# Every third half-unit of the second layer's first half takes a score bank and the attention bank for its sums

## The chip, the cores and the metric

The kernel runs on one core of one Trainium2 chip. The metric is the device time of one execution in microseconds. Five engines work side by side, each through its own instruction stream in order: TensorE (PE, its weight loads PEld), VectorE (DVE), ScalarE (ACT), GpSimd (POOL) and SyncE (SP, which issues the transfers).

## The reference

Attention with RMS-normed q and k (4 batches, 12 heads, 448 positions, head size 64), then two feed-forward layers over the 1792 tokens; what matters for the change is the last one:

```python
def _moe2_ref(x, w_in, w_out):      # x 1792x768, w_in 768x2048, w_out 2048x768
    h = x @ w_in
    g = h * np.cos(h)
    return (g @ w_out).astype(np.float32)
```

## The kernel before, in words

The work comes in stages: attention of batch 0, then gate, val and out1 of the first layer for batch after batch with the attention of the next batch threaded in, then the second layer in two halves: "h" (`x @ w_in` with `h cos h`) and "out2" (`g @ w_out`). Every operand of the second layer is kept as a pair of fp16 parts, high and low, so each 128x128 block of weights costs three matmuls of 448 columns (L1002 to L1004: high x high, high x low, low x high).

The loop of the h half (L1265 to L1294) runs over 8 pieces `c` of 256 columns of `w_in` and, inside, over 4 batches `b`. One pass of the inner loop is called a **half-unit** here: 256 output columns of one batch, as two banks of PSUM (`f` = 0 and 1), 36 matmuls in all. There are 32 half-units, in the order c, b, and four of them with one `c` are called a group. PSUM has eight banks: four in the pool `ps_m` (tiles "mm"), three score banks in `ps_s` (tiles "s"), one attention bank in `ps_t` (tile "t"); the names s and t are of the attention, which is over by then. A half-unit takes two mm banks (L1269), so its banks come round again two half-units later.

What reads the banks is `fin_h` (L1123 to L1149), for each of the two banks: ACT rounds to a whole multiple (L1134), DVE takes off the multiple of two pi in two steps (L1140 and L1141, the first reads the bank), ACT takes the absolute value and the sine (L1142, L1143), DVE multiplies by the bank (L1144, the last reader of the bank), ACT and POOL split the product into two fp16 parts (L1148, L1149). The bank is free when L1144 is done.

Beside this the loop prepares weights. At `b == 3` it converts the next `w_in` pieces from their 64-bit form (`conv64`: L841, L842, L843 on DVE), takes their squares (L861 on ACT) and splits a piece that is already scaled (L873 on ACT, L874 on DVE). At `b == 1` `w_scale` adds the squares up across partitions with a tiny matmul (L868, in a bank of `ps_s`). From the half-unit (5, 3) on, `pre_step` converts the last pieces of `w_out` in the same way, one for each half-unit, and at (7, 1) `out2_scales` sets the scales with which out2's weights are split (L930 on ACT, L931 on DVE, from `raw` tiles that are loaded back from DRAM, `raw<-o`). Out2 (L1297 on) takes its banks from all three pools: s, s, s, t, mm, mm, mm, and its matmuls are L1015.

The order on each engine is not the program's: the kernel is built with a scheduler that walks through the program with a timing model and lets an instruction that is ready go ahead of an earlier one. Tiles of one pool are handed out in the program's order. So a change of the banks moves instructions on every engine.

```python
ps_t = ... tile_pool(name="ps_t", bufs=1, space=PSUM)     # L175
ps_s = ... tile_pool(name="ps_s", bufs=3, space=PSUM)     # L176
ps_m = ... tile_pool(name="ps_m", bufs=4, space=PSUM)     # L1194
```

Of the kernel before, what the change touches and what calls it, by code (L numbers as in the profile page):

```python
# [140 lines left out]
def kernel(ctx: ExitStack, tc, q, k, v, g_q, g_k, w_gate, w_val, w_out, w2_in, w2_out, out):  # L141
# [33 lines left out]
    ps_t = ctx.enter_context(tc.tile_pool(name="ps_t", bufs=1, space=PSUM))  # L175
    ps_s = ctx.enter_context(tc.tile_pool(name="ps_s", bufs=3, space=PSUM))  # L176
# [7 lines left out]
    def xy_tile(more=False):  # L184
        return xy_pools[more].tile([P, 2, S], F16, tag="xy", name="xy")
# [4 lines left out]
    def bank(pool, tag):  # L190
        return pool.tile([P, 512], F32, tag=tag, name=tag)
# [707 lines left out]
    def w_loads(upto):  # L899
        while nload[0] <= min(upto, len(pieces) - 1):  # L900
            pc = pieces[nload[0]]
            if (pc["kind"] == "out1" and not pc["fresh"] or pc["kind"] == "out2" and pc["fresh"]) and nload[0] > upto - LA + LO:
                return
            w_load(nload[0])
            nload[0] += 1

    def w_conv(j):
        if j >= len(pieces) or not pieces[j]["fresh"] or pieces[j]["kind"] == "out2":
            return
        pc = pieces[j]  # L910
        w32_t[j] = conv64(raw_t.pop(j))
        if pc["kind"] != "out1":
            squares(unit_of(pc), w32_t[j])

    def w_scale(j):
        if j < len(pieces) and pieces[j]["fresh"] and pieces[j]["last"] and pieces[j]["kind"] in ("gate", "val", "h"):
            unit_scale(unit_of(pieces[j]))

    def w_split(j):
        if j >= len(pieces) or not (pieces[j]["fresh"] or pieces[j]["kind"] == "out1"):  # L920
            return
        pc = pieces[j]
        if pc["kind"] == "out2":
            wp_full[j] = []
            for kk in range(2):
                kt = pc["k0"] + kk
                w32 = w32_t.pop((j, kt))
                so = oscl[:, kt:kt + 1]
                wp = wp_tile(F16)
                nc.scalar.activation(wp[:, 0], w32, AF.Copy, scale=so)  # L930
                nc.vector.scalar_tensor_tensor(wp[:, 1], w32, so, wp[:, 0], op0=ALU.mult, op1=ALU.subtract)  # L931
                wp_full[j].append(wp)
                for o in range(H * D // CO):
                    dst = scr["out2", o, pc["k0"]].rearrange("p a x -> p (a x)").rearrange("p (k a f) -> p k a f", k=2, a=2)
                    stores.append((dst[:, kk], wp[:, :, o * CO:(o + 1) * CO]))
            wp_t[j] = None
            return
        w32 = w32_t.pop(j)
        dst = scr[pc["key"]]
        if pc["kind"] == "out1":  # L940
            wh, wl = wp_tile(F32R), wp_tile(F32R)
            nc.scalar.activation(wh, w32, AF.Copy)  # L942
            nc.gpsimd.tensor_sub(wl, w32, wh.bitcast(F32))  # L943
            if pc["fresh"]:
                stores.append((dst, w32))
            wp_t[j] = (wh, wl)
        else:
            wp = split16(unit_of(pc), w32)
            if pc["kind"] != "h":
                stores.append((dst, wp))  # L950
            wp_t[j] = (wp[:, 0], wp[:, 1])

    def w_store():
        while stores:
            dst, src = stores.pop(0)
            nc.sync.dma_start(dst, src)
# [6 lines left out]
    def pre_step(more=True):  # L963
        done = False
        if pre_split and (pre_split[0][0] == "out2" or len(pre_split) > 1):
            kind, c, k0, w32 = pre_split.pop(0)
            if kind == "h":
                for kind, c, k0, w32 in ((kind, c, k0, w32), pre_split.pop(0)):
                    stores.append((scr[kind, c, k0], split16(UNIT0[kind] + c, w32)))
            done = True  # L970
        if pre_scale and (pre_scale[0][0] == "out2" or len(pre_scale) > 1):
            kind, c, k0, w32 = pre_scale.pop(0)
            unit_scale(UNIT0[kind] + c)
            if kind == "h":
                pre_split.append((kind, c, k0, w32))
                pre_split.append(pre_scale.pop(0))
            done = True
        if pre_conv:
            kind, c, k0, rw = pre_conv.pop(0)
            w32 = conv64(rw)  # L980
            squares(UNIT0[kind] + c, w32)
            if kind == "out2":
                stores.append((o32[c // 2][:, c % 2 * 768:(c % 2 + 1) * 768], w32))
            pre_scale.append((kind, c, k0, w32))
            done = True
        if pre_load and more:
            kind, c, k0 = pre_load.pop(0)
            rw = load64(w2_out, c, 0, 1, 768) if kind == "out2" else load64(w2_in, k0, c, 3, 256)
            pre_conv.append((kind, c, k0, rw))
            done = True  # L990
        return done


    def mm_piece(j, ps, rhs):
        pc = pieces[j]
        n, first, last = pc["n"], pc["first"], pc["last"]
        wh, wl = wp_t[j]
        for i in range(n):
            x = rhs(pc["k0"] + i)
            for f in range(2):  # L1000
                s = slice(i * 256 + f * P, i * 256 + (f + 1) * P)
                nc.tensor.matmul(ps[f][:, :S], wh[:, s], x[:, 0], start=(first and i == 0), stop=False)  # L1002
                nc.tensor.matmul(ps[f][:, :S], wh[:, s], x[:, 1], start=False, stop=False)  # L1003
                nc.tensor.matmul(ps[f][:, :S], wl[:, s], x[:, 0], start=False, stop=(last and i == n - 1))  # L1004
# [61 lines left out]
    def y_scale(b):  # L1066
        n = nm_p.tile([P, 4], F32, tag="nm", name="nm")
        nc.vector.tensor_reduce(n[:, 0:1], ynrm[:, b * KX:(b + 1) * KX], axis=AX.X, op=ALU.add)
        ps = bank(ps_s, "s")
        nc.tensor.matmul(ps[:, :1], full, n[:, 0:1], start=True, stop=True)  # L1070
        pow2_scale(ps[:, :1], ysc[:, B + b:B + b + 1], ysc[:, b:b + 1])
        ts = nc.vector.tensor_scalar
        sy, yi = ysc[:, b:b + 1], ysc[:, B + b:B + b + 1]
        ts(yhi[:, b, 0:1], yi, 1.0 / TWO_PI, None, op0=ALU.mult)
        ts(yhi[:, b, 1:2], yi, -1.0, None, op0=ALU.mult)
        ts(yhs[:, b, 0:1], sy, -PI_HI, None, op0=ALU.mult)
        ts(yhs[:, b, 1:2], sy, -PI_LO, None, op0=ALU.mult)
# [5 lines left out]
    def y_split(b, kt):  # L1083
        if kt == 0:
            y_scale(b)
        sy = ysc[:, b:b + 1]
        t = yt.pop((b, kt))
        x = Y[b, kt] = xy_tile(b < 2)
        xv = x.rearrange("p a (q t) -> p a q t", t=NS)
        tv = t.rearrange("p (t q) -> p q t", t=NS)  # L1090
        nc.scalar.activation(xv[:, 0], tv, AF.Copy, scale=sy)
        nc.vector.scalar_tensor_tensor(xv[:, 1], tv, sy, xv[:, 0], op0=ALU.mult, op1=ALU.subtract)
# [101 lines left out]
    ps_m = ctx.enter_context(tc.tile_pool(name="ps_m", bufs=4, space=PSUM))  # L1194
# [11 lines left out]
    for b in range(B):  # L1206
# [14 lines left out]
        for qn in range(per):  # L1221
# [22 lines left out]
            if pc["last"]:  # L1244
                def fin(kind=kind, b=b, c=c, ps=cur[0]):
                    fins[kind](b, c, ps)
# [15 lines left out]
        deferred.pop(0)()  # L1262
    for kt in range(KX):
        y_split(B - 1, kt)
    for c in range(NH):  # L1265
        j0 = j
        j += 2
        for b in range(B):
            ps = [bank(ps_m, "mm") for _ in range(2)]  # L1269
            if b == 1 and c:  # L1270
                w_scale(j0 + 3)
            for jj in range(j0, j):
                w_store()
                if b == 3:
                    w_split(jj + 2)
                    w_conv(jj + 4)
                    w_loads(min(jj + 6, N2 - 1))
                mm_piece(jj, ps, lambda kt: Y[b, kt])
                if late:
                    late.pop(0)[1]()  # L1280
            if (c, b) >= HPRE:
                pre_step()
            if (c, b) == (NH - 1, 1):
                while pre_step():
                    w_store()
                out2_scales()
                w_loads(N2 + 3)

            def fin(b=b, c=c, ps=ps):
                fins["h"](b, c, ps)  # L1290
            if not (b == B - 1 and c == NH - 1):
                late.append((0, fin))
            else:
                fin()  # L1294
    nt = 2 * S // P
    seq = 0
    while j < len(pieces):  # L1297
        ps = [None] * nt
# [49 lines left out]
```

## Time and profile before

| what | value |
|---|---|
| median of 3 runs | 1356.93 us (1356.93 to 1362.55) |
| the profiled execution | 1358.27 us, of which 1356.5 us are its span |
| busy share of the span | PE 88%, DVE 65%, ACT 50%, POOL 35% |
| mean granted TensorE clock | 0.953 of full speed |
| the h half in the trace | about 891 to 1140 us |
| out2 in the trace | 1140 us to the end, its first matmuls from 1101 us |

A busy PE in these tables is not PE at its peak: matmuls overlap, one of 448 columns is shown as 0.35 us long, while they start 0.19 us apart. Idle time is therefore read from the starts of the matmuls.

### The profile page before, as it was taken

To read this page: it belongs to the slowest core of one execution; us is meant where nothing else is said; L and a number is where in the kernel's file an instruction comes from. 1 tells how busy PE (TensorE), PEld (TensorE's weight loads), DVE (VectorE), ACT (ScalarE), POOL (GpSimd) and SP (SyncE) were. 2 spreads that over 40 slices of the span, in tenths; PEclk is the share of its full clock that TensorE was granted. 3 is DMA by queue.
4 is the path that set the end of the run, shared out by engine and by line. 5 is a ranking of instruction groups with operands and counts; after the bars stand their busy time and mean duration, and the time that the engine had idled before them with its cause. 6 is when DMAs were issued, how large, how long until landed. Compare 5 with 4: busy or idle time off the path is not lost.

```text
span 1356.5 us, 18241 instructions
## 1 busy us (share of the span) xinstructions
PE 1199.2 (88%) x6454; PEld 676.3 (50%) x6454; DVE 883.3 (65%) x1556; ACT 684.4 (50%) x1318; POOL 474.5 (35%) x351
## 2 busy tenths in 40 slices
PE   0588787878799978999999998979998999999998
PEld 0233343334574435854458655955444555666665
DVE  7868968999967787647763399477889875100000
ACT  2567577775435556445664365456767776100000
POOL 8621335555733456623554013503323332000000
PEclk9889798788899999999999999989999999999999
DMA  7535559987999976789867688641113222633121
GB/s 239 142 82 143 175 149 241 242 215 216 244 327 276 219 170 157 194 231 203 187 131 191 217 305 292 233 160 48 47 47 129 82 82 70 212 110 100 58 88 41
DMA packets 255195, 227.02 MB, mean 167 GB/s; under 512 B 177280, under 2 KB 205952, under 8 KB 255104
## 3 DMA queue, kind: packets, MB, share of 16 engines
q1 hardware_dynamic: 255104, 225.86, 59.3%
q8 instruction: 50, 0.82, 0.3%
q14 instruction: 41, 0.34, 0.1%
HBM read 147.13 MB, written 38.77 MB: 137 GB/s over the span
## 4 chain that ended last, share of the span: by engine, by line
PE 45%; DVE 19%; DMA 6%; ACT 4%; issue 3%; POOL 1%; SPq 0%; DVEq 0%; ACTq 0%; POOLq 0%
PE mm L1002 9%; PE mm L1003 8%; PE mm L1004 8%; PE mm L1015 7%; PE s L1015 7%; DMA T<-h 3%; PE t L1015 2%; DVE w L842 2%; DVE w L843 2%; PE t L555 2%; DVE w L841 2%; DMA PT<-p 2%; DVE tmp L1140 1%; PE s L444 1%; DVE sm L453 1%
## 5 line engine op out<-in xcount | busy, mean ns | idle before, releaser
L1002 PE MATMUL mm<-xy,wp 128*128 128x448 f16 x960 | 347.4, 363 | 35.9 <-DVE tmp L1144 12.2
L1003 PE MATMUL mm<-xy,wp 128*128 128x448 f16 x960 | 347.9, 362 | 0.0
L1004 PE MATMUL mm<-xy,wp 128*128 128x448 f16 x960 | 342.7, 362 | 2.2 <-DVE wp L874 2.1
L1015 PEld LDWEIGHTS <-g 128*128 128x128 f16 x1344 | 131.5, 98 | 87.2
L1002 PEld LDWEIGHTS <-wp 128*128 128x128 f16 x960 | 97.9, 102 | 120.9 <-issue 25.9
L1003 PEld LDWEIGHTS <-wp 128*128 128x128 f16 x960 | 96.3, 100 | 108.9 <-issue 33.5
L1004 PEld LDWEIGHTS <-wp 128*128 128x128 f16 x960 | 94.9, 100 | 98.5 <-issue 10.3
L1149 POOL TENSOR_TENSOR g<-tmp,g 128x448 f16<-128x448 f32 x64 | 73.7, 1165 | 188.3 <-ACT g L1148 188.3
L496 POOL TENSOR_TENSOR p<-pr,p 128x448 f16<-128x448 f32 x72 | 89.9, 1252 | 140.9 <-ACT p L487 122.2
L943 POOL TENSOR_TENSOR wp<-w,wp 128x768 fp32r<-128x768 f32 x48 | 96.3, 2010 | 79.7 <-ACT wp L942 50.2
L463 ACT ACTIVATE pr<-s,sm,esc 128x448 f32<-128x448 f32 x126 | 90.2, 718 | 60.0 <-DVE sm L457 56.8
L1002 PE MATMUL mm<-g,wp 128*128 128x448 f32 x288 | 108.6, 378 | 0.0
L1003 PE MATMUL mm<-g,wp 128*128 128x448 f32 x288 | 107.2, 372 | 0.0
L1004 PE MATMUL mm<-g,wp 128*128 128x448 f32 x288 | 106.7, 371 | 0.2 <-POOL wp L943 0.2
L1050 POOL TENSOR_TENSOR g<-tmp,g 128x448 fp32r<-128x448 f32 x48 | 63.8, 1343 | 108.7 <-ACT g L1049 108.5
L1015 PE MATMUL s<-wp,g 128*128 128x384 f16 x576 | 100.1, 326 | 0.0
L1015 PE MATMUL mm<-wp,g 128*128 128x384 f16 x576 | 99.1, 326 | 0.0
L453 DVE TENSOR_REDUCE sm<-s 128x1 f32<-128x448 f32 x126 | 75.5, 615 | 20.2 <-PE s L444 19.9
L487 ACT ACTIVATE p<-pr 128x448 f16<-128x448 f32 x126 | 70.0, 570 | 28.1 <-DMA PT<-p 27.1
L321 POOL TENSOR_TENSOR ri<-ss,half 128x14 f32<-128x14 f32 x24 | 64.5, 2692 | 47.1 <-DVE ss L319 39.3
L1160 ACT ACTIVATE tmp<-mm,osc 128x384 f32<-128x384 f32 x8 | 4.7, 581 | 148.6 <-PE mm L1015 147.8
L842 DVE SCALAR_TENSOR_TENSOR w<-raw,w 128x768 int32<-128x768 int32 x68 | 76.6, 1138 | 0.8
(170 smaller groups left out, 2078.0 us busy)
## 6 DMA issues: line engine op xcount, KB each, us to landing
raw<-in_moe_w_out_dram SPq DMA_DIRECT2D x28, 768.0 KB, 5.2
wp<-scr_gate SPq DMA_DIRECT2D x36, 384.0 KB, 4.4
wp<-scr_val SPq DMA_DIRECT2D x36, 384.0 KB, 4.7
w<-scr_out SPq DMA_DIRECT2D x36, 384.0 KB, 4.0
raw<-in_moe_w_in_dram SPq DMA_DIRECT2D x16, 768.0 KB, 4.7
raw<-in_moe_w_gate_dram SPq DMA_DIRECT2D x12, 768.0 KB, 5.5
raw<-in_moe_w_val_dram SPq DMA_DIRECT2D x12, 768.0 KB, 5.0
wp<-scr_out SPq DMA_DIRECT2D x24, 384.0 KB, 3.0
```

The costliest lines, as they stand in the source:

```text
L321: nc.gpsimd.tensor_tensor(ri.rearrange("p a b -> p (a b)"), ss, half[:, :2 * NS], op=ALU.pow)
L453: nc.vector.tensor_reduce(sm[:, 0, t:t + 1], slot[n][:, :S], axis=AX.X, op=ALU.max)
L463: nc.scalar.activation(e, slot.pop(n)[:, :S], AF.Exp, bias=sm[:, 1, t:t + 1], scale=esc, accum_out=sm[:, 2, t:t + 1],)
L487: nc.scalar.activation(hi, slot[n], AF.Copy)
L496: eng.tensor_sub(p16[:, t - t0, 1], slot.pop(n), p16[:, t - t0, 0])
L842: nc.vector.scalar_tensor_tensor(wi, hi, -0x40000000, wi, op0=ALU.bitwise_and, op1=ALU.bitwise_or)
L943: nc.gpsimd.tensor_sub(wl, w32, wh.bitcast(F32))
L1002: nc.tensor.matmul(ps[f][:, :S], wh[:, s], x[:, 0], start=(first and i == 0), stop=False)
L1003: nc.tensor.matmul(ps[f][:, :S], wh[:, s], x[:, 1], start=False, stop=False)
L1004: nc.tensor.matmul(ps[f][:, :S], wl[:, s], x[:, 0], start=False, stop=(last and i == n - 1))
L1015: nc.tensor.matmul(ps[:, :CO], x[:, a, p0:p0 + P], rhs, start=st, stop=sp)
L1149: nc.gpsimd.tensor_sub(x[:, 1], r, x[:, 0])
```

## The change

```diff
@@ -1262,11 +1262,13 @@
         deferred.pop(0)()
     for kt in range(KX):
         y_split(B - 1, kt)
+    nh = 0
     for c in range(NH):
         j0 = j
         j += 2
         for b in range(B):
-            ps = [bank(ps_m, "mm") for _ in range(2)]
+            ps = [bank(ps_s, "s"), bank(ps_t, "t")] if nh % 3 == 2 else [bank(ps_m, "mm") for _ in range(2)]
+            nh += 1
             if b == 1 and c:
                 w_scale(j0 + 3)
             for jj in range(j0, j):
```

Half-units are numbered 0 to 31 by `nh`. Numbers 2, 5, 8, ... take a score bank and the attention bank, the others two mm banks. Every pair of banks then comes round three half-units later instead of two. No instruction is added or taken away; the lines of the loop move down by two. The scheduler makes another order of it, on all engines, from the third half-unit on; ahead of it the orders are alike. Three places:

**PE, start of the h half**, from the last matmul of half-unit 1 (`mm_8598` is its second bank; `s_9113` and `s_9389` are the cross-partition sums of the weights' squares). Before:

```order
L1004 MATMUL mm_8598<-xy_7805,wp_8383 128x448
L868 MATMUL s_9113<-nm_8979,full_98 128x1
L868 MATMUL s_9113<-nm_9028,full_98 128x1
L868 MATMUL s_9389<-nm_9252,full_98 128x1
L1002 LDWEIGHTS wp_8381
L1002 MATMUL mm_8660<-xy_7857,wp_8381 128x448
```

Now:

```order
L1004 MATMUL mm_8598<-xy_7805,wp_8383 128x448
L1002 LDWEIGHTS wp_8381
L1002 MATMUL s_8660<-xy_7857,wp_8381 128x448
L1003 LDWEIGHTS wp_8381
L1003 MATMUL s_8660<-xy_7857,wp_8381 128x448
```

The sums are gone from this place, and half-unit 2 goes to a bank of its own. The two sums of `s_9113` now stand ahead of half-unit 9, those of `s_9389` ahead of half-unit 13; between half-units 2 and 3 stand 14 matmuls of half-unit 5 (`s_8849`).

**DVE, the weights' work of one group.** Before, with the end of half-unit 11 (`mm_9243`, `mm_9244` are its banks):

```order
L874 SCALAR_TENSOR_TENSOR wp_9797<-w32_9524,wsc_100,wp_9797 128x768
L1140 SCALAR_TENSOR_TENSOR tmp_9353<-tmp_9349,ht_9346,mm_9243 128x448
L841 TENSOR_SCALAR w32_9852<-raw_9582 128x768
L1140 SCALAR_TENSOR_TENSOR tmp_9361<-tmp_9351,ht_9346,mm_9244 128x448
L1141 SCALAR_TENSOR_TENSOR tmp_9353<-tmp_9349,ht_9346,tmp_9353 128x448
L842 SCALAR_TENSOR_TENSOR w32_9852<-raw_9582,w32_9852 128x768
L874 SCALAR_TENSOR_TENSOR wp_9849<-w32_9576,wsc_100,wp_9849 128x768
L1141 SCALAR_TENSOR_TENSOR tmp_9361<-tmp_9351,ht_9346,tmp_9361 128x448
L843 SCALAR_TENSOR_TENSOR w32_9852<-raw_9582,w32_9852 128x768
L1144 SCALAR_TENSOR_TENSOR tmp_9353<-tmp_9353,mm_9243 128x448
L841 TENSOR_SCALAR w32_10076<-raw_9806 128x768
L1144 SCALAR_TENSOR_TENSOR tmp_9361<-tmp_9361,mm_9244 128x448
```

Now, with half-unit 13 (`mm_9387`, `mm_9388`), the second of its group; the two splits (L874) stand ahead of it, with half-unit 12:

```order
L841 TENSOR_SCALAR w32_9800<-raw_9530 128x768
L1140 SCALAR_TENSOR_TENSOR tmp_9485<-tmp_9481,ht_9478,mm_9387 128x448
L842 SCALAR_TENSOR_TENSOR w32_9576<-raw_9306,w32_9576 128x768
L1140 SCALAR_TENSOR_TENSOR tmp_9493<-tmp_9483,ht_9478,mm_9388 128x448
L842 SCALAR_TENSOR_TENSOR w32_9800<-raw_9530,w32_9800 128x768
L1141 SCALAR_TENSOR_TENSOR tmp_9485<-tmp_9481,ht_9478,tmp_9485 128x448
L843 SCALAR_TENSOR_TENSOR w32_9576<-raw_9306,w32_9576 128x768
L1141 SCALAR_TENSOR_TENSOR tmp_9493<-tmp_9483,ht_9478,tmp_9493 128x448
L843 SCALAR_TENSOR_TENSOR w32_9800<-raw_9530,w32_9800 128x768
L1144 SCALAR_TENSOR_TENSOR tmp_9485<-tmp_9485,mm_9387 128x448
L1140 SCALAR_TENSOR_TENSOR tmp_9557<-tmp_9553,ht_9550,s_9458 128x448
```

The same conversions are done later against the matmuls (the tile `w32_9800` stood with half-unit 7 before and stands with half-unit 13 now), and they are gathered behind the first two half-units of a group instead of its last.

**PE, where out2 begins** (`s_10806` is its first bank, `g2_8630` the first block of g). Before, behind half-unit 24:

```order
L1002 LDWEIGHTS wp_10123
L1002 MATMUL mm_10153<-xy_7557,wp_10123 128x448
L1003 LDWEIGHTS wp_10123
L1003 MATMUL mm_10153<-xy_7557,wp_10123 128x448
L1004 LDWEIGHTS wp_10123
L1004 MATMUL mm_10153<-xy_7557,wp_10123 128x448
L1015 LDWEIGHTS g2_8630
L1015 MATMUL s_10806<-wp_10694,g2_8630 128x384
```

Now, behind half-unit 31, the last:

```order
L1002 MATMUL mm_10693<-xy_8556,wp_10432 128x448
L1003 LDWEIGHTS wp_10432
L1003 MATMUL mm_10693<-xy_8556,wp_10432 128x448
L1004 LDWEIGHTS wp_10432
L1004 MATMUL mm_10693<-xy_8556,wp_10432 128x448
L1015 LDWEIGHTS g2_8630
L1015 MATMUL s_10806<-wp_10694,g2_8630 128x384
```

Before, 24 of out2's matmuls on score banks and 6 on the attention bank stood among the h half-units 25 to 31; now none does. The last cross-partition sum of `w_out`'s squares, which stood ahead of the second bank of half-unit 21 before, now stands between half-units 29 and 30, and the splits of out2's weights, which began on DVE with half-unit 23, now begin with half-unit 29. SP's order of transfers is the same but for one pair that changes places.

## Rows read from the trace of the kernel before

**Rows 1.** Engines by stretch: span, busy us (instructions) by engine, granted clock, DMA share, GB/s.
```profile
core 0: us, PE busy (x) PEld busy (x) DVE busy (x) ACT busy (x) POOL busy (x), PEclk, DMA share, GB/s
904.40:912.40 8.00, 1.09 (x7) 0.94 (x7) 7.75 (x16) 5.76 (x11) 0.00 (x0) 0.72 0.28 89
912.40:922.20 9.80, 9.76 (x37) 4.37 (x37) 4.18 (x9) 4.95 (x9) 4.00 (x4) 0.70 0.03 10
922.20:1020.00 97.80, 91.58 (x485) 47.44 (x483) 83.33 (x139) 68.15 (x121) 28.63 (x25) 1.00 0.15 49
1020.00:1060.00 40.00, 35.20 (x191) 18.84 (x190) 39.67 (x76) 30.16 (x55) 13.10 (x10) 1.00 0.38 139
1060.00:1140.00 80.00, 80.00 (x430) 42.01 (x429) 56.08 (x109) 57.83 (x98) 25.83 (x24) 1.00 0.17 59
1140.00:1353.00 213.00, 213.00 (x1312) 128.08 (x1309) 21.49 (x29) 22.32 (x33) 2.12 (x3) 1.00 0.32 104
```

**Rows 2.** PE's waits, 890 to 1145 us: in total us, times, longest.
```profile
PE mm L1002 <- DVE tmp L1144: 12.2, 12, 3.1
PE s L868 <- ACT raw L861: 5.8, 2, 3.9
```

**Rows 3.** PE in order of time: start, us, instruction [idle before, releaser].
```profile
904.40 0.50 PE L868 MATMUL s<-nm,full 128*128 128x1 f32 x4
908.78 0.59 PE L868 MATMUL s<-nm,full 128*128 128x1 f32 x2 [3.88 <-ACT raw L861]
912.44 0.53 PE L1002 MATMUL mm<-xy,wp 128*128 128x448 f16 x1 [3.07 <-DVE tmp L1144]
...
918.30 0.35 PE L1003 MATMUL mm<-xy,wp 128*128 128x448 f16 x1
...
966.62 0.38 PE L868 MATMUL s<-nm,full 128*128 128x1 f32 x2 [1.88 <-ACT raw L861]
967.24 0.35 PE L1002 MATMUL mm<-xy,wp 128*128 128x448 f16 x1 [0.24 <-DVE tmp L1144]
...
974.05 0.28 PE L868 MATMUL s<-nm,full 128*128 128x1 f32 x2
974.19 0.35 PE L1002 MATMUL mm<-xy,wp 128*128 128x448 f16 x1
...
995.00 0.35 PE L1004 MATMUL mm<-xy,wp 128*128 128x448 f16 x1
997.35 0.35 PE L1002 MATMUL mm<-xy,wp 128*128 128x448 f16 x1 [2.00 <-DVE tmp L1144]
```

**Rows 4.** The h half's costliest groups, 904 to 1140 us: count, busy us, mean ns, idle before.
```profile
L1141 DVE SCALAR_TENSOR_TENSOR tmp<-tmp,ht 128x448 f32<-128x448 int32 x62 | 42.4, 704 | 0.1
L1140 DVE SCALAR_TENSOR_TENSOR tmp<-tmp,ht,mm 128x448 f32<-128x448 int32 x63 | 41.0, 671 | 14.9 <-ACT tmp L1134 14.9
L1144 DVE SCALAR_TENSOR_TENSOR tmp<-tmp,mm 128x448 f32<-128x448 f32 x62 | 38.3, 618 | 27.9 <-ACT tmp L1143 27.3
...
L842 DVE SCALAR_TENSOR_TENSOR w<-raw,w 128x768 int32<-128x768 int32 x13 | 12.8, 988 | 0.1
...
L874 DVE SCALAR_TENSOR_TENSOR wp<-w,wsc,wp 128x768 f16<-128x768 f32 x10 | 10.9, 1087 | 0.0
...
L841 DVE TENSOR_SCALAR w<-raw 128x768 int32<-128x768 int32 x12 | 8.6, 715 | 0.2 <-DMA o<-w 0.2
...
L931 DVE SCALAR_TENSOR_TENSOR wp<-raw,oscl,wp 128x768 f16<-128x768 f32 x5 | 5.1, 1024 | 1.0 <-ACT wp L930 1.0
...
L930 ACT ACTIVATE wp<-raw,oscl 128x768 f16<-128x768 f32 x5 | 4.6, 922 | 0.0
```

**Rows 5.** ACT and DVE in order of time, start of the h half.
```profile
907.79 0.84 ACT L861 ACTIVATE raw<-w 128x768 f32<-128x768 f32 x1 [2.21 <-DVE w L843]
...
912.42 0.62 DVE L1144 SCALAR_TENSOR_TENSOR tmp<-tmp,mm 128x448 f32<-128x448 f32 x1
```

**Rows 6.** Transfers issued 850 to 1145 us: count, KB each, median us to landing.
```profile
raw<-o SPq DMA_DIRECT2D x5, 768.0 KB, 4.6
...
scr_out<-wp SPq DMA_DIRECT2D x12, 192.0 KB, 2.0
```

## The prediction

> **What bounds the kernel now.** I read the table of stretches first: it tells where TensorE stands still. From 1060 us to the last matmul it is busy all the time, 80.00 of 80.00 and 213.00 of 213.00 us, at the full clock (1.00, 2.4 GHz) [rows 1]. So from there on nothing but fewer matmuls would help, and the change keeps their number. Between 904 and 1060 us it is not: 1.09 of 8.00 us, then a stretch with the clock down, then 91.58 of 97.80 and 35.20 of 40.00 us [rows 1]. The table of waits says who is to blame: 12 stops, 12.2 us, for L1144, the last reader of a bank, and 5.8 us for ACT's squares L861, which the small sums L868 need [rows 2]. That is the pattern of a producer with two pairs of banks. The half-unit that comes two later must wait until DVE is through.
>
> What these stops cost is read from starts. 36 matmuls and their half-unit take 974.05 - 967.24 = 6.81 us, 0.189 us each, and the next half-unit follows two sums 0.14 us later [rows 3]. A row is 0.35 us long, so a stop costs some 0.16 us more than its idle figure: from 995.00 to 997.35 are 2.35 us instead of 0.19, a loss of 2.16 where the row says 2.00 [rows 3].
>
> **The loss before, which is the most there is to win.**
> 1. Start of the h half: 904.40 to 912.44 us are 8.04 us in which PE does six sums [rows 3]. At 0.14 us for two these are 0.42 us, and they are still to be done. Loss 7.6 us.
> 2. Behind this stop the granted clock is a mean of 0.70, that is, half speed (1.2 GHz) for a while [rows 1]. 16 matmuls take 918.30 - 912.44 = 5.86 us [rows 3] instead of 16 x 0.189 = 3.02. Loss 2.8 us.
> 3. Later stops: 97.80 - 91.58 = 6.2 and 40.00 - 35.20 = 4.8 us [rows 1], together 11.0, and 0.16 us more for each of 11 stops, 1.8. Loss 12.8 us.
>
> Together 23.2 us.
>
> **The change, part by part.**
>
> *Start.* By the order, PE goes from half-unit 1 straight to half-unit 2 on the two new banks, which nobody holds. It starts at 904.4 instead of 912.44 and lasts 6.8 us, to 911.2. Then come 14 matmuls of half-unit 5, 14 x 0.189 = 2.6 us, to 913.9. Only then does half-unit 3 need the banks of half-unit 0. Before, these were free at 912.42 + 0.62 = 913.04 us [rows 5], and now not later: the conversion's L861, which came 2.21 us late and ran ahead of the sines on ACT [rows 5], has left this place. So no stop remains, and without the stop the clock has no reason to fall. Gain 7.6 + 2.8 = 10.4 us. If I am wrong by a microsecond or two here, the stop is short, and stops of 2 us later in this stage leave the clock at 1.00 [rows 1, 3].
>
> *The moved sums.* The same sums stand later now, two in a row at the head of a group's second half-unit. The squares they add were taken a half-unit or more earlier. At 0.14 us for two they cost what they did. A score bank that a sum takes was last held three requests of that pool earlier. Taken at nothing; the bound above is under rivals.
>
> *The later stops.* Is DVE fast enough once PE does not wait? For one group it does 4 x 2 x (0.671 + 0.704 + 0.618) = 15.9 us of fin_h, 2 x (0.715 + 2 x 0.988) = 5.4 of conversions (L843 counted as L842) and 2 x 1.087 = 2.2 of splits [rows 4]: 23.5 us, and small ones, against 4 x 6.81 + 0.14 = 27.4 us of PE. So DVE is not the bound on average, but the weights' work comes in a burst. Before, 4.0 + 5.4 + 2.2 = 11.6 us stood with one half-unit, and there was one half-unit of 6.8 us to hide the excess: that is the loss of 2.16 us at 997.35 [rows 3]. Now the splits and one L841 stand with a group's first half-unit (4.0 + 2.2 + 0.7 = 6.9 us) and the rest with its second (4.0 + 4.7 = 8.7 us). Counted from the end of the first half-unit's matmuls, DVE begins some 0.7 us later and has both done after 0.7 + 15.6 = 16.3 us; with the small ones, the sums' scaling and waits for ACT some 18 to 19. The second half-unit's banks are wanted by the half-unit three further, 3 x 6.81 + 0.14 = 20.6 us after. Spare: some 2 us, where before there was a lack of 2.
>
> I do not take this for the whole truth, because DVE was busy for 39.67 of 40.00 us between 1020 and 1060 [rows 1], and a saturated engine does not give back every stop. Bound from below: with the spare, nothing is lost. Bound from above: each of the five bursts (groups from half-units 8, 12, 16, 20 and 24) loses what one loses at 997.35, 5 x 2.16 = 10.8 us. I take 0.7 us for each, 3.5 us, nearer the lower end, since the third pair gives 6.8 us and the lack was 2.16. Gain 12.8 - 3.5 = 9.3 us.
>
> *End of the h half.* Out2's 30 matmuls that stood among the last half-units now stand behind them: the same number. But the cover for out2's weights is gone. Their scales hang on the last sum, now ahead of half-unit 30; from there PE has two half-units, 13.6 us. Two splits for the first piece are 2 x 0.922 on ACT and 1.024 on DVE behind them [rows 4], some 3 us, and perhaps 2 for the scales. Spare 8 us. Later pieces: out2 uses one in 42 matmuls, 42 x 213.00/1312 = 6.8 us [rows 1], and one is loaded in 4.6 us [rows 6] into one of two buffers while the other is split. Taken at nothing. If a wait for L1144 vanishes, the next thing that could be late is a load of `raw`, and it is not.
>
> **Sum.** 10.4 + 9.3 = 19.7 us. The profiled execution took 1358.27 us, of which 1356.5 are the span; that gives 1338.6. The median of the runs, 1356.93, lies 1.3 us lower, so I forecast **1337.3 us**.
>
> **Rivals.**
> - *The bursts still stop PE.* For it: DVE at 99% in 1020 to 1060 us [rows 1]. The five bursts at the upper bound take 10.8 instead of 3.5 us: 1344.6, and one fall of the clock (2.8) more, 1347.4. Against: the third pair is worth more than the lack. Chance 0.22.
> - *The change does not do what it says*, because the sums use the score banks too and PE, in order, stands at a sum whose bank is still being read. At 1.88 us, the one such wait inside the stage [rows 3], for each of the ten sums, 19 us: 1356, no change. Against: by the order the bank a sum takes was left by DVE a half-unit earlier. Chance 0.06.
> - *Slower: out2's weights come too late.* SP issues the load of the next `raw` behind the stores of the piece before, which wait for L931. If the two buffers do not overlap, a piece takes 4.6 + 2 x 0.922 + 2 x 1.024 + 2.0 (stores) = 10.5 us [rows 4, 6] against 6.8. Then PE waits some 8 us for the first of the eight and 3.7 for each other, 34 us: 1337.3 + 34 = 1371. It is slower by over 0.5% from 27 us of waiting on. Against: the order of SP is as before and out2 never waited [rows 1]; for it: before, three pieces were ready early. Chance 0.04.
> - *Slower: the clock.* Before, PE stopped at bank turns at every few half-units for up to 2 us, and the granted clock stayed at 1.00 from 922 us on; only the stop of 8 us was followed by half speed [rows 1, 3]. If short stops at each of the ten turns to the third pair did lower it, ten times 2.8 us would make 28: 1365. Chance 0.03. The Trainium skill, in "TensorE: Matmul & The Clock Gate", section "A second HAM failure mode: psum-queue depth-cycling", tells of a kernel in which cycling through PSUM banks makes PE pause so often that its clock goes up and down. By that rule more banks in turn would cost time; this trace speaks against it, with the clock at 1.00 over all the short stops.
>
> **How the numbers follow.** A change of 0.5%, 6.8 us, is about what a measurement of this kernel can tell from none. The forecast, with the lower bound of the bursts and a few microseconds above, has 0.65 (1333.7 to 1342). The low end is all of the 23.2 us, 1333.7. The high end takes in the first rival, 1347.4. Forecast and first rival together have 0.87, and some of it lies over the end. Faster by over 0.5% (below 1350.1) is 0.87, the same 0.06, slower 0.07.
>
> **What would show it.** PE busy in nearly every microsecond from the start of the h half to the end; no wait for L1144 over 2 us, their sum under 4 (12.2 before); no stop in front of half-unit 2 and no half speed behind it; DVE at 95% or more from half-unit 8 to 27. I am wrong at the bursts if L1144 still has five waits of 2 us; wrong at the end if PE's first long wait is for L930 or L931; and wrong altogether if a sum L868 waits for a bank.

## The result and the profile after

The changed kernel takes 1343.39 us (median of four, 1340.91 to 1344.76) where the kernel before took 1359.34 in the runs beside it. The ratio is 0.9874, with a 95% interval from 0.9854 to 0.9894: faster by 1.1 to 1.5%, clear of the noise. The forecast was 1337.3 with a range from 1333.7 to 1347.4, so the time lies inside the range, 6.1 us above the number.

The profiled execution took 1340.91 us, 17.36 less than the one before. Not all of this is the change. The h half begins at these rows (the first matmul behind out1, start and duration, PE in order of time), first of the kernel before, then of the changed one:

```profile
891.20 0.36 PE L1002 MATMUL mm<-xy,wp 128*128 128x448 f16 x1
...
1351.92 1.14 PE L1015 MATMUL t<-wp,g 128*128 128x384 f16 x6
```
```profile
885.95 0.36 PE L1002 MATMUL mm<-xy,wp 128*128 128x448 f16 x1
...
1334.31 1.14 PE L1015 MATMUL t<-wp,g 128*128 128x384 f16 x6
```

The second row of each is its last matmul group. The order of the instructions up to the h half is the same in both (three matmuls of the h half stand earlier, among those of out1), and yet the profiled execution of the changed kernel was 5.25 us ahead at its start. From that start to the end of the last matmul are 1351.92 + 1.14 - 891.20 = 461.86 us before and 449.50 after. I call this stretch **the length** from here on. It fell by 12.4 us, and the experiments are read by it.

The engines by stretch in the changed kernel (columns as in [rows 1]):

```profile
904.40:912.40 8.00, 8.00 (x45) 4.12 (x43) 6.40 (x14) 7.75 (x14) 2.66 (x3) 1.00 0.00 0
912.40:922.20 9.80, 9.80 (x53) 5.08 (x52) 7.50 (x12) 7.31 (x13) 4.20 (x4) 1.00 0.00 0
922.20:1020.00 97.80, 97.80 (x525) 51.37 (x524) 80.00 (x148) 72.50 (x129) 30.35 (x28) 1.00 0.14 41
1020.00:1060.00 40.00, 40.00 (x217) 21.21 (x216) 33.16 (x61) 29.20 (x54) 13.09 (x12) 1.00 0.29 99
1060.00:1125.00 65.00, 58.22 (x301) 29.92 (x299) 52.55 (x112) 49.05 (x86) 19.39 (x17) 0.95 0.41 134
1125.00:1335.00 210.00, 210.00 (x1295) 126.45 (x1293) 17.05 (x22) 17.98 (x26) 1.66 (x2) 1.00 0.31 101
```

Up to 1060 us TensorE is busy all the time at the full clock, where it lost 23.2 us before [rows 1]. But between 1060 and 1125 us, where it did not wait at all before [rows 1], it now stands still for 6.78 us and the clock is down for a while. PE's waits and its stops in order of time say where:

```profile
PE mm L1015 <- DVE tmp L1144: 3.8, 1, 3.8
PE s L868 <- ACT raw L861: 2.7, 3, 1.2
PE mm L1002 <- DVE tmp L1144: 0.3, 1, 0.3
```
```profile
1072.53 0.38 PE L868 MATMUL s<-nm,full 128*128 128x1 f32 x2 [1.02 <-ACT raw L861]
1080.22 0.38 PE L868 MATMUL s<-nm,full 128*128 128x1 f32 x2 [0.48 <-ACT raw L861]
1081.48 0.35 PE L1002 MATMUL mm<-xy,wp 128*128 128x448 f16 x1 [0.29 <-DVE tmp L1144]
1089.07 0.38 PE L868 MATMUL s<-nm,full 128*128 128x1 f32 x2 [1.19 <-ACT raw L861]
...
1096.32 0.38 PE L868 MATMUL s<-nm,full 128*128 128x1 f32 x2
...
1110.18 3.09 PE L1015 MATMUL s<-wp,g 128*128 128x384 f16 x18
...
1118.01 4.00 PE L1015 MATMUL mm<-wp,g 128*128 128x384 f16 x12 [3.77 <-DVE tmp L1144]
1121.81 3.86 PE L1015 MATMUL s<-wp,g 128*128 128x384 f16 x17
1125.50 1.14 PE L1015 MATMUL mm<-wp,g 128*128 128x384 f16 x6
1126.48 0.33 PE L1015 MATMUL s<-wp,g 128*128 128x384 f16 x1
...
1127.61 3.09 PE L1015 MATMUL mm<-wp,g 128*128 128x384 f16 x18
1130.54 0.65 PE L1015 MATMUL s<-wp,g 128*128 128x384 f16 x3
```

Four short stops (2.98 us, and 0.16 us each beside the idle figure: 3.6) stand at sums and one bank turn. One of 3.77 us (3.9) stands at out2's start, and behind it the clock is half for a while: 12 + 17 + 6 = 35 matmuls take 1126.48 - 1118.01 = 8.47 us, at the later rate of 2.93 / 18 = 0.163 us 5.7, a loss of 2.8. Together 10.3 us. 23.2 less 10.3 are 12.9, and the length fell by 12.4.

What holds out2's start is not the bank's own work. The rows of SP, ACT and DVE ahead of it (a fence for each engine):

```profile
1107.50 1.98 SPq L956 DMA_DIRECT2D scr_out<-wp  x4
1109.53 0.49 SPq L883 DMA_DIRECT2D raw<-o  x1
```
```profile
1115.26 0.93 ACT L930 ACTIVATE wp<-raw,oscl 128x768 f16<-128x768 f32 x1 [1.49 <-DMA raw<-o]
1116.10 0.56 ACT L1142 ACTIVATE tmp<-tmp 128x448 f32<-128x448 f32 x1
1116.56 1.40 ACT L1143 ACTIVATE tmp<-tmp,hpi,ht 128x448 f32<-128x448 f32 x2
```
```profile
1106.45 1.95 DVE L931 SCALAR_TENSOR_TENSOR wp<-raw,oscl,wp 128x768 f16<-128x768 f32 x2
...
1116.22 1.02 DVE L931 SCALAR_TENSOR_TENSOR wp<-raw,oscl,wp 128x768 f16<-128x768 f32 x1 [2.47 <-ACT wp L930]
1117.34 1.27 DVE L1144 SCALAR_TENSOR_TENSOR tmp<-tmp,mm 128x448 f32<-128x448 f32 x2
```

The load of out2's third piece is issued at 1109.53, when L931 has freed a `raw` and the stores of the first piece are out. It lands 5.7 us later: ACT stands at L930 for it until 1115.26, with L1142 and L1143 of half-unit 30 in its queue behind; DVE stands at L931 until 1116.22, with L1144 of half-unit 30 behind. PE waits for that L1144's bank.

Two more places, half-unit for half-unit, tell what the third pair did. At the start, the banks of half-unit 0 are free no sooner than before. Their last reader in the changed kernel:

```profile
906.39 1.27 DVE L1144 SCALAR_TENSOR_TENSOR tmp<-tmp,mm 128x448 f32<-128x448 f32 x2 [0.34 <-ACT tmp L1143]
```

Counted from the start of the h half they are free at 906.39 + 1.27 - 885.95 = 21.7 us, where it was 913.04 - 891.20 = 21.8 before [rows 5], although the sums and the squares L861 have left this place. PE is through with half-unit 1 at 13.2 us in both. With two pairs it would have had to wait.

It is the same at a burst. The last matmul of half-unit 11 before and the last reader of its first bank, then those of half-unit 13 now, and the first matmul of half-unit 16, which takes that bank next:

```profile
987.62 0.35 PE L1004 MATMUL mm<-xy,wp 128*128 128x448 f16 x1
996.69 0.61 DVE L1144 SCALAR_TENSOR_TENSOR tmp<-tmp,mm 128x448 f32<-128x448 f32 x1
```
```profile
981.40 0.35 PE L1004 MATMUL mm<-xy,wp 128*128 128x448 f16 x1
991.50 0.61 DVE L1144 SCALAR_TENSOR_TENSOR tmp<-tmp,mm 128x448 f32<-128x448 f32 x1
995.21 0.35 PE L1002 MATMUL mm<-xy,wp 128*128 128x448 f16 x1
```

The bank is free 9.7 us behind the start of the last matmul before and 10.7 us behind it now. With two pairs it is wanted one half-unit later, after some 6.8 us, and PE stopped (997.35 in [rows 3]); with three, two half-units lie between, and PE comes at 13.8 us.

### The profile page after: what moved, and what is told of

Read it like the earlier page. It is cut to its first block, busy times and chain, and to the rows that moved or that the text cites. A ratio compares the mean times of both kernels' runs of the same rounds, so it can differ in the third digit from the quotient of the medians.

```text
span 1339.1 us, 18253 instructions
## 1 busy us (share of the span) xinstructions
PE 1191.8 (89%) x6454; PEld 673.1 (50%) x6454; DVE 880.0 (66%) x1556; ACT 681.0 (51%) x1318; POOL 471.9 (35%) x351
## 4 chain that ended last, share of the span: by engine, by line
PE 36%; DVE 19%; ACT 9%; DMA 8%; issue 5%; POOL 1%; SPq 1%; ACTq 0%; DVEq 0%; POOLq 0%
PE mm L1015 7%; PE s L1015 7%; PE mm L1002 6%; PE mm L1004 5%; PE mm L1003 5%; DMA PT<-p 3%; DMA T<-h 3%; DVE w L842 2%; PE t L1015 2%; ACT tmp L1143 2%; ACT tmp L1142 2%; DVE tmp L1140 2%; DVE tmp L1141 2%; DVE w L841 2%; DVE w L843 1%
## 5 line engine op out<-in xcount | busy, mean ns | idle before, releaser
L1002 PE MATMUL mm<-xy,wp 128*128 128x448 f16 x840 | 302.7, 361 | 22.8 <-ACT wp L873 8.9
L1003 PE MATMUL mm<-xy,wp 128*128 128x448 f16 x840 | 302.7, 360 | 0.0
L1004 PE MATMUL mm<-xy,wp 128*128 128x448 f16 x840 | 298.7, 360 | 2.6 <-DVE wp L874 2.4
L453 DVE TENSOR_REDUCE sm<-s 128x1 f32<-128x448 f32 x126 | 75.4, 615 | 19.7 <-PE s L444 19.5
L841 DVE TENSOR_SCALAR w<-raw 128x768 int32<-128x768 int32 x68 | 49.6, 739 | 47.9 <-POOL wp L943 21.1
L842 DVE SCALAR_TENSOR_TENSOR w<-raw,w 128x768 int32<-128x768 int32 x68 | 80.2, 1190 | 0.7
```

The costliest lines, as they stand in the source:

```text
L453: nc.vector.tensor_reduce(sm[:, 0, t:t + 1], slot[n][:, :S], axis=AX.X, op=ALU.max)
L841: nc.vector.tensor_scalar(wi, hi, 3, 0x3FFFFFF8, op0=ALU.logical_shift_left, op1=ALU.bitwise_and)
L842: nc.vector.scalar_tensor_tensor(wi, hi, -0x40000000, wi, op0=ALU.bitwise_and, op1=ALU.bitwise_or)
```

## The experiments

In the table, idle is PE's waiting from the h half on, and the last column counts the stretches at half speed behind a stop. "Start" is where the h half began in the profiled execution. The ratio is to the kernel before in the same round of runs, where its median was 1358.01 (again, only_first, no_first, to_21), 1358.90 (from_17, w32_piece, sums_late, w32_sums_late) or 1360.02 (the last four). The length comes from one profile each; the changed kernel's two differ by 0.9 us, so that a difference of under 1 us in length says nothing.

| kernel | median us | ratio to before (95%) | start | length | idle for L1144 | idle at sums | half speed |
|---|---|---|---|---|---|---|---|
| before | 1359.34 | | 891.20 | 461.86 | 12.2 | 5.8 | 1 |
| changed | 1343.39 | 0.9874 (0.9854 to 0.9894) | 885.95 | 449.50 | 4.1 | 2.7 | 1 |
| again | 1343.70 | 0.9895 (0.9877 to 0.9913) | 889.17 | 448.63 | 4.4 | 2.7 | 1 |
| only_first | 1353.40 | 0.9960 (0.9947 to 0.9974) | 894.14 | 456.00 | 7.8 | 4.3 | 2 |
| no_first | 1343.63 | 0.9893 (0.9873 to 0.9912) | 888.15 | 449.14 | 4.5 | 2.5 | 1 |
| from_17 | 1348.97 | 0.9924 (0.9902 to 0.9947) | 893.32 | 453.67 | 6.0 | 5.4 | 1 |
| to_21 | 1346.26 | 0.9919 (0.9897 to 0.9942) | 886.80 | 449.52 | 2.9 | 4.0 | 2 |
| w32_piece | 1343.74 | 0.9884 (0.9861 to 0.9906) | 890.64 | 445.77 | 2.5 | 3.0 | 0 |
| sums_late | 1340.57 | 0.9864 (0.9841 to 0.9886) | 889.96 | 445.47 | 2.2 | 2.1 | 1 |
| w32_sums_late | 1343.14 | 0.9885 (0.9860 to 0.9909) | 896.24 | 444.95 | 1.9 | 2.3 | 1 |
| early_out2 | 1343.52 | 0.9867 (0.9840 to 0.9894) | 889.03 | 444.74 | 2.5 | 2.5 | 0 |
| early_out2_sums_late | 1344.00 | 0.9881 (0.9855 to 0.9907) | 893.90 | 447.88 | 6.4 | 0 | 1 |
| early_out2_all | 1343.02 | 0.9871 (0.9842 to 0.9899) | 892.81 | 444.93 | 4.1 | 0 | 1 |
| before_early_out2 | 1360.41 | 0.9998 (0.9982 to 1.0014) | 893.55 | 462.11 | 12.0 | 5.8 | 2 |

The lengths add up. 461.86 less the prediction's 23.2 leaves 438.7 us without any stop; with the idle time of a row, 0.16 us for each of its stops, and 1.7 to 2.8 us for each stretch at half speed, every changed kernel's length comes out within 1 us.

**again**: the changed kernel unaltered.

> The changed kernel once more, to part its gain into stages. Theory: all of the gain arises in the h half and at out2's start (23.2 us of stops before, some 10 us of new ones: about 13 us), and the 5.25 us by which the profiled execution was ahead at the first matmul of the h half are a matter of the single execution. Then that start lies between 886 and 891 us here, and from there to the last matmul are about 449.5 us again. Rival: moving the banks also changes the stages before; then the start lies at 886 us again.

The start lay at 889.17, inside what the theory allowed; the length was 448.63. The rival, 886 again, falls. Over all fourteen profiles the start lies between 885.95 and 896.24 with the same instructions ahead of it, a spread of 10.3 us, so single executions can't rank kernels that differ by less.

### Where the gain at the start and in the bursts comes from

**only_first**

```diff
-ps = [...] if nh % 3 == 2 else [...]
+ps = [...] if nh == 2 else [...]
```

> The third pair is used once, by half-unit 2, and never again. Theory: the banks remove the stop of 7.6 us at the start and the half clock of 2.8 behind it; the later stops for L1144 come back (12.8 us), and the new waits at the end (sums 3.4, out2's start 6.7) go. From the first matmul of the h half to the last: 461.9 - 10.4 = 451.5 us, the time about 10 us under the kernel before. Rival (a stop that is only put off): half-unit 3 then stops for the banks of half-unit 1 or the half clock comes anyway, and the time is within 4 us of the kernel before.

Its waits:

```profile
PE mm L1002 <- DVE tmp L1144: 7.8, 10, 2.0
PE s L868 <- ACT raw L861: 4.3, 3, 2.1
```

The length is 456.00, 4.5 us over the forecast; the median is 4.6 us under that of the kernel before, where theory had 10 and the rival under 4. The stop at the start went: half-unit 3 waited 0.63 us. But the first later sum stopped for 2.12 us, another for 1.89, and both were followed by half speed, where I had expected the later stops to cost what they did before. The bursts stay, as expected. Using the third pair once made the length 5.9 us shorter.

**no_first**

```diff
-ps = [...] if nh % 3 == 2 else [...]
+ps = [...] if nh % 3 == 2 and nh > 2 else [...]
```

> The third pair is used from half-unit 5 on, not by half-unit 2. Theory (the banks make the gain at the start): PE stops for 7 to 8 us in front of half-unit 2 and runs at half clock behind it, 10.4 us lost, all else as in the changed kernel: some 10 us slower than it, within 5 us of the kernel before. Rival (the gain at the start comes from the order in which the scheduler puts sums and the conversion): the start stays without a stop, and the time is that of the changed kernel.

By the numbers the rival is right: the length is the changed kernel's. But the edit doesn't test its mechanism. At the place where PE stood before, this kernel runs a pair on the two banks too:

```profile
901.16 0.35 PE L1004 MATMUL mm<-xy,wp 128*128 128x448 f16 x1
901.36 0.35 PE L1002 MATMUL s<-xy,wp 128*128 128x448 f16 x1
```

It is half-unit 5, the first that has the third pair here; the scheduler pulls it ahead. So the edit did not take away what it should have, and my forecast overlooked that the scheduler fills the hole with whatever has free banks.

**from_17**

```diff
-ps = [...] if nh % 3 == 2 else [...]
+ps = [...] if nh % 3 == 2 and nh >= 17 else [...]
```

> The third pair is used from half-unit 17 on; nothing at the start can run on it. (The kernel without half-unit 2's use had half-unit 5 at that place instead, on the same two banks, and no stop.) Theory: the start is as in the kernel before, a stop of 7 to 8 us with a bank turn behind the sums and half clock behind it, 10.4 us lost, and one or two bursts of about 2 us before half-unit 17 come back; the waits at the end stay as in the changed kernel. From the first matmul of the h half to the last: 449 + 10 to 14 = 459 to 463 us, the time that of the kernel before within 4 us. Rival (the start's stop hung on the order of sums and conversion, which this kernel's order also has as before, but the h half hides it): under 455 us.

Now the start is as before, with PE's stops and, as the last row, the first matmul at the full clock again:

```profile
910.90 0.38 PE L868 MATMUL s<-nm,full 128*128 128x1 f32 x2 [3.88 <-ACT raw L861]
914.56 0.53 PE L1002 MATMUL mm<-xy,wp 128*128 128x448 f16 x1 [3.28 <-DVE tmp L1144]
...
918.21 0.35 PE L1003 MATMUL mm<-xy,wp 128*128 128x448 f16 x1
```

The stop is the 7.6 us of the prediction. Half speed behind it cost less: ten matmuls take 918.21 - 914.56 = 3.65 us instead of 1.89, a loss of 1.8 where the prediction has 2.8. With no_first this shows that the start's stop goes when a pair on free banks, of whichever half-unit, stands at this place. The sums and the squares move together with it in each of these kernels (the conversion's L841 to L843 stay where they were on DVE), and moving them alone wasn't tried. But the banks of half-unit 0, free at 21.7 to 21.8 us with them and without, show that moving them would not have been enough. The length, 453.67, is under the theory's 459 all the same, for two reasons that it did not have: no burst came back, though half-unit 17 is the first on the third pair (the matmuls of such half-units are pulled ahead in pieces of 8 to 20, from 72 us behind the start of the h half on, and fill the holes), and at the end the clock did not fall.

### What was lost at the end

**to_21**

```diff
-ps = [...] if nh % 3 == 2 else [...]
+ps = [...] if nh % 3 == 2 and nh < 21 else [...]
```

> The third pair is used up to half-unit 20 only. Theory (the new waits at the end, 3.4 us in sums that wait for squares and 6.7 at out2's start, come from the h half's last turns of the third pair, which push the last sums and out2's first work back): start and bursts keep their gain up to half-unit 20 or so, out2's start stops less or not at all, and the time is 4 to 8 us under the changed kernel, less up to 4 us for the stops for L1144 that come back behind half-unit 24. Rival (DVE is simply full and hands its delay on to whatever stands at the end): stops for L1144 come back in the same sum, and the time is that of the changed kernel within 2 us.

The theory fails and the rival is nearer: no stop at out2's start, but a sum (4.0 us) and the bank turns (2.9) have it, and the length is 449.52, the changed kernel's. The median is 2.9 us above the changed kernel's; the interval overlaps that of again and lies just above that of the first four runs, so a small loss is not excluded. Its two longest stops on PE:

```profile
1048.72 0.38 PE L868 MATMUL s<-nm,full 128*128 128x1 f32 x2 [4.00 <-ACT raw L861]
...
1060.14 0.49 PE L1002 MATMUL mm<-xy,wp 128*128 128x448 f16 x1 [2.00 <-DVE tmp L1144]
```

**w32_piece** (lines behind 885 are 4 higher)

```diff
-if pc["kind"] == "out2" and pc["fresh"]:
+if pc["kind"] == "out2" and pc["fresh"] and j == N2 + 2:
+    for kk in range(2):
+        w32_t[j, pc["k0"] + kk] = w32_p.tile([P, 768], F32, tag="w32", name="w32")
+        nc.sync.dma_start(w32_t[j, pc["k0"] + kk], o32[pc["k0"] // 2][:, kk * 768:(kk + 1) * 768])
+elif pc["kind"] == "out2" and pc["fresh"]:
```

> The third fresh piece of out2's weights is loaded early into two tiles of its own, not behind the stores into a buffer that two pieces share. Theory (the stop of 3.8 us at out2's start comes from VectorE's L931, which waits for that late load and stands ahead of the last bank's L1144): the stop and the half clock behind it go, 6.7 us; from the first matmul of the h half to the last 442 to 444 us. Rival (VectorE is late at that place anyway, with the scales and four splits): the stop stays over 2 us and the length over 447 us.

The order on PE and DVE is the same, the load is early, and on ACT one L930 of that piece now stands ahead of both L1142 of half-unit 30 instead of between them. PE at out2's start, then DVE ahead of it:

```profile
1120.54 2.11 PE L1019 MATMUL mm<-wp,g 128*128 128x384 f16 x12 [1.48 <-DVE tmp L1148]
1125.81 1.14 PE L1019 MATMUL mm<-wp,g 128*128 128x384 f16 x6 [1.04 <-DVE tmp L1148]
```
```profile
1118.49 1.00 DVE L935 SCALAR_TENSOR_TENSOR wp<-w,oscl,wp 128x768 f16<-128x768 f32 x1
1119.87 1.27 DVE L1148 SCALAR_TENSOR_TENSOR tmp<-tmp,mm 128x448 f32<-128x448 f32 x2 [0.37 <-ACT tmp L1147]
```

The first stop fell from 3.8 to 1.48 us, the half speed went, a second of 1.04 came. The length fell by 3.3 against the mean of the changed kernel's two profiles (449.07), half of the 6.7 forecast. The late load, with that place on ACT, was the larger part of the stop; the rest is DVE, which has L935 (L931 in the other kernels) and the scales ahead of the bank's last reader.

**sums_late**

```diff
-if pre_scale and (pre_scale[0][0] == "out2" or len(pre_scale) > 1):
+if pre_scale and (len(pre_scale) > 1 or pre_scale[0][0] == "out2" and not (pre_late and pre_conv)):
```

(`pre_late` is filled when the h half begins.)

> Four of out2's five last sums stand one half-unit later in TensorE's order, so their squares have 6.8 us more; the last sum stays where it is. Theory (the three stops of 2.7 us, 3.4 with what a stop costs beside its idle time, are only the place of a sum behind squares that ScalarE does at the end of the same half-unit): they go, out2's start stays as it is, the length is 445.5 to 447 us. Rival (the squares are late because VectorE and the loads are, and slip along): stops of the same sum at the new places, or a longer one at the two sums that now stand together ahead of half-unit 30, and 449 us or more.

Its two long stops on PE:

```profile
1077.76 0.35 PE L1002 MATMUL mm<-xy,wp 128*128 128x448 f16 x1 [1.63 <-DVE tmp L1144]
...
1100.52 0.38 PE L868 MATMUL s<-nm,full 128*128 128x1 f32 x2 [2.15 <-ACT raw L861]
```

The length, 445.47, is at the theory's lower end; the way there isn't the theory's. The stops did not go, they were put together (1.63 at a bank turn, 2.15 at the last sum, as the rival had it), and half speed followed. What went, but for 0.64 us, is the stop at out2's start: in this kernel's order on DVE L931 of the third piece stands behind L1144 of half-unit 30, at 1122.98 and 1118.74.

**w32_sums_late**: both edits.

> Both edits of the two kernels before. Theory: the two losses are independent, 3.4 + 6.7 = 10 us; the length is 439 to 441 us, all but free of stops, and the time some 10 us under the changed kernel (about 1333). Rival (one full engine hands its delay on): no better than the better of the two by more than 1 us.

444.95, 0.5 us less than the better one, and the median is 1343.14. They don't add up, as the rival said.

**early_out2**

```diff
-HPRE = (5, 3)
+HPRE = (5, 2)
```

(`HPRE` is the half-unit, as (c, b), from which on the preparation of out2's weights goes along.)

> The preparation of out2's weights (load, conversion, squares, sum, one step for each half-unit) starts one half-unit earlier, in half-unit 22 instead of 23, so the last sum stands ahead of half-unit 29 and out2's scales and splits have 20 us instead of 13.6 in front of out2's first matmul. Theory (what was lost at the end is preparation that comes one half-unit too late): the stop at out2's start goes with the half clock behind it (6.7 us); the sums still stand right behind their squares and keep about 1 us each. From the first matmul of the h half to the last: 442 to 444 us. Rival (VectorE has no room for it earlier either): L1144 gets stops of 2 us and more around half-units 24 to 27 and the length is 447 us or more.

444.74, 4.3 us less than the changed kernel's mean and 0.7 us over the theory's upper end; out2 stops once, for 1.94 us at the last bank of its first piece, without half speed. The rival's stops did not come.

**early_out2_sums_late**: this and the edit of sums_late.

> The preparation starts one half-unit earlier, and the sums are put one half-unit behind their squares: they stand where they stand in the changed kernel, the squares 6.8 us ahead of them. Theory: the stops at the sums go (3.4 us), the scales are no earlier than in the changed kernel, so out2's start can still stop for up to 3.8 us: 441 to 446 us in length, by whether the third piece's load comes earlier with the last conversion. Rival (one full engine hands its delay on): 448 us or more.

No sum stops any more, and the length is 447.88: over the theory's 446, all but the rival's 448, and only 1.2 us less than the changed kernel's. What the sums gave, out2's start took; its row on PE, then DVE ahead:

```profile
1124.82 4.00 PE L1015 MATMUL mm<-wp,g 128*128 128x384 f16 x12 [5.65 <-DVE tmp L1144]
```
```profile
1123.03 1.02 DVE L931 SCALAR_TENSOR_TENSOR wp<-raw,oscl,wp 128x768 f16<-128x768 f32 x1 [2.44 <-ACT wp L930]
1124.14 1.27 DVE L1144 SCALAR_TENSOR_TENSOR tmp<-tmp,mm 128x448 f32<-128x448 f32 x2
```

DVE reaches this L1144 1124.14 - 893.90 = 230.2 us behind the start of the h half; in the changed kernel it is 1117.34 - 885.95 = 231.4. PE came 3.0 us sooner (its first `t` matmuls of out2 end at 1118.03 + 1.14 - 893.90 = 225.3 instead of 1113.11 + 1.14 - 885.95 = 228.3) and waited for nearly the same moment. The stops at the sums are therefore not a loss of their own in the changed kernel: it is the chain of scales, first splits, late load and L931 that ends last, and PE waits here or there.

**early_out2_all**: early_out2_sums_late ("the kernel before" in the text below) with the early load of w32_piece.

> As the kernel before, and the third fresh piece is loaded early into tiles of its own. Theory: no stop over 1.5 us is left in the h half or at out2's start, 439 to 442 us in length, and the time 8 us or more under the changed kernel's 1343.5. Rival: the same as without the early load within 1 us.

444.93. The theory's "no stop over 1.5 us" falls: out2's start stops for 3.40 us, and DVE reaches the bank's last reader (L1148 here) at 1120.72 - 892.81 = 227.9 us, 2.3 us earlier than without the early load. The rival falls too: the length is 3.0 us less.

**before_early_out2**: the kernel before with HPRE = (5, 2).

> The kernel before, without the third pair, with the preparation of out2's weights one half-unit earlier. Theory (before, the loss lies in bank turns for L1144 and at the start, not in out2's preparation): its stops for L1144 stay at about 12 us and its time within 3 us of the kernel before. Rival (the work that stands in VectorE's bursts matters more than the banks): 4 us or more faster.

As the theory: 0.9998, the same stops, 462.11.

None of the versions is measured to be faster than the change: from w32_piece to early_out2_all their lengths are 1 to 4 us shorter, but their intervals overlap the change's two. The shortest median, 1340.57 of sums_late, is 3 us below.

## Why the prediction came out as it did

- **Start, 10.4 us: right.** PE runs through 904 to 922 us at the full clock, and from_17 has the stop and the half speed back. Half-unit 3 did not wait, and half-unit 0's banks were free no later than before, as worked out.
- **Bursts, 12.8 less 3.5: the mechanism right, the rest too cautious.** (The later stops were twelve, not eleven; that is 0.2 us.) PE was busy for 97.80 of 97.80 and 40.00 of 40.00 us; all 12.8 were gained. The spare in the working was enough, and the 0.7 us for each burst was not needed. That it was the third pair and not the scheduler's other order of DVE's work is shown by the bank at half-unit 13, free no sooner than before; a kernel with this order and two pairs was not run. Between 1020 and 1060 us the gain is mixed with another: half of the conversions that stood there moved behind 1060 us (next point).
- **DVE at 95% or more: wrong.** It has 80.00 of 97.80 us. I read 39.67 of 40.00 [rows 1] as a full engine. Part of the preparation of out2's weights, which the scheduler had pulled into that stretch, now stands later (six conversions were begun there before, three now), so the stretch was full by order and not by need.
- **The moved sums, "taken at nothing": wrong.** "The squares they add were taken a half-unit or more earlier" holds for the sums of the h weights. For out2's, ACT does the squares behind the L1134 of the half-unit that PE has just ended, and PE stands at the sum right behind: 1.02, 0.48 and 1.19 us.
- **The end of the h half, "taken at nothing": the step that cost most, 6.7 us.** "The next thing that could be late is a load of `raw`, and it is not": it was, by the load of the third piece. I counted 8 us of spare for the first piece: 13.6 from the last sum to out2, less 3 for the splits and 2 for the scales. The 13.6 came true (1096.32 to 1110.18 us is 13.9), but the splits ended on DVE at 1106.45 + 1.95 = 1108.40, 12.1 us behind the sum, because the steps from the sum to the scales stand in DVE's queue among those of fin_h; 1.8 us were left. For each later piece I set 6.8 us against 4.6 of loading. I did not follow the third piece, whose buffer is free only when the first is split, nor see what stands behind its split in ACT's and DVE's queues: L1143 and L1144 of half-unit 30, whose bank out2 needs. That is the mechanism of the third rival, once and small instead of at every piece. The load isn't all of it: with it early, in w32_piece, 3.3 of the 6.7 us came back.
- **The sum.** 19.7 forecast, 12.4 measured in the length: 3.5 more in the bursts, 3.6 lost at sums and 6.7 at out2's start, 0.5 unexplained. The runs' ratios, 0.9874 and 0.9895, make 14 to 17 us, with some 2.5 us of uncertainty each. Of the 6.1 us by which the time lies above the number, 2.4 are the kernel before, which took 1359.34 in these runs and not 1356.93. That the time lies inside the range is in part luck: it is above the 1342 up to which I gave the forecast 0.65, in the part that I had added for bursts that still stop PE, and these did not occur; the loss came from the end, which I had taken at nothing.
- **The signs.** The start without a stop or half speed came as said, and so did the bursts without a stop. The longest wait for L1144 was 3.8 us instead of at most 2, their sum 4.1 instead of under 4. "Wrong at the end if PE's first long wait is for L930 or L931" names the right place; the wait itself is booked on the L1144 that stands behind L931.
- **The rivals.** Nothing of the first, second and fourth occurred. The second's price, 1.88 us for a wait for a bank, was misread: that row's releaser is L861, the squares. On the fourth: the clock stayed at 1.00 over all the turns to the third pair from 904 to 1060 us, and there was no stop at a turn. The page of the Trainium skill named there ("TensorE: Matmul & The Clock Gate", section "A second HAM failure mode: psum-queue depth-cycling") tells of a kernel that cycles through PSUM banks and in which PE idles so often between groups of matmuls that its clock goes up and down. This trace shows no such idle in that stretch, so it doesn't test what the page tells; it shows that one pair of banks more in turn need not bring such idles.

## What to carry to other kernels

A third pair of banks paid here as work that PE can do while the others wait, whichever half-unit takes it; but when the stops are gone, PE reaches the next stage earlier, and the preparation that hung behind those stops, on loads above all, is what to cost next. Follow each late load to the in-order queue where its first reader stands, and list what stands behind that reader. And read an engine's busy share in a stretch together with what of it could have stood elsewhere.

## What the runs showed of the hardware

**Half speed after short stops.** I had taken from [rows 1, 3] that stops of 2 us leave the clock alone. In the fourteen profiles, from the h half on, all nine places with a stop of 3.07 us or more had half speed (1.2 GHz) in the stop or just behind it, none of the eighteen stops from 1.02 to 1.63 us did, and of thirteen from 1.88 to 2.15 us six did. The same sum with the same wait of 1.88 us, in the kernel before and in before_early_out2 (7 us each, columns as in [rows 1]):

```profile
966.62:973.62 7.00, 6.76 (x36) 3.63 (x37) 6.69 (x16) 6.51 (x13) 2.77 (x2) 1.00 0.60 186
```
```profile
967.54:974.54 7.00, 6.76 (x27) 3.24 (x28) 6.07 (x15) 5.01 (x10) 2.77 (x2) 0.76 0.66 180
```

Of the first 7 us behind the same sum, 36 matmuls were done in one execution and 27 in the other: the half speed cost nine matmuls of 0.189 us, 1.7 us. What decides between the two cases the runs don't show.

**The spread of the start.** In the first 885 us the mean granted clock of an execution was 0.93 to 0.95. The six with 0.93 began the h half at 891.2 to 896.2 us, the four with 0.95 at 886.8 to 889.2, the four with 0.94 at 886.0 to 893.6. TensorE was busy for 746 to 750 us there in each. The slowest group has the least clock, so part of the spread goes with the time at half speed in the stages ahead; but at 0.94 alone the starts lie 7.6 us apart, so it is not all of it, and that it is a cause was not tested.
